# Chunked attention and a two-layer block: pairs of tiles instead of triples, softmax with a maximum, V turned on TensorE

## The chip, the cores and the metric

The kernel runs on one core of a Trainium2 chip. The metric is the device time of one execution in microseconds. TensorE multiplies matrices and transposes through a matmul with an identity; VectorE (DVE), ScalarE (ACT) and GpSimd (POOL) work on elements; POOL and SyncE (SP) also issue the DMA transfers. Every engine works through its own list of instructions in the order of the program, and waits at an instruction until what it reads or overwrites is free.

## The reference

Inputs are q, k, v of shape (4, 8, 768, 64), eight memory keys and values for each batch and head, a scale vector and two weight matrices, all in float32.

```python
chunk, left_ctx, right_ctx = (32, 16, 8)
scale = 1.0 / np.sqrt(D)
for c in range(nc):                       # 24 chunks of 32 queries
    c_start = c * chunk
    c_end = c_start + chunk
    l_start = max(0, c_start - left_ctx)
    r_end = min(S, c_end + right_ctx)
    k_full = np.concatenate([mem_k, k[:, :, l_start:r_end]], axis=2)
    v_full = np.concatenate([mem_v, v[:, :, l_start:r_end]], axis=2)
    scores = scale * np.matmul(q[:, :, c_start:c_end], k_full.transpose(0, 1, 3, 2))
    scores = scores - np.max(scores, axis=-1, keepdims=True)
    a = np.exp(scores)
    a = a / (np.sum(a, axis=-1, keepdims=True) + 1e-09)
    out[:, :, c_start:c_end] = np.matmul(a, v_full)
x = out.transpose(0, 2, 1, 3).reshape(B, S, H * D)      # (4, 768, 512)
xn = (x - mean(x)) / np.sqrt(var(x) + 1e-06) * g_ln
return x + np.maximum(xn @ w_ch1, 0.0) @ w_ch2          # hidden width 2048
```

A chunk of 32 queries sees 16 keys ahead of it, its own 32, 8 behind it, and 8 memory keys: 64 in all.

## The kernel before, in words

The 4 x 768 rows are 24 tiles of 128 rows, six for each batch. A tile is two groups of 64 rows, four chunks. An octet is eight neighbouring rows: loaded as one run of 512 numbers into one partition.

**Loads.** `load_kq` brings k and q of a batch in octets (2 KB runs). V is loaded row by row (256-byte runs) by `load_v_group` (L106) or `load_v_head` (L112); the 16 rows ahead of a group and the 8 behind it are copied from one partition to another by `v_before` and `v_after` on SP. All HBM loads stand in POOL's list, with the element work that POOL does. The weights come through `load_w1` and `load_w2`; `scale_w1` (L154) multiplies w1 by the scale vector on VectorE.

**Attention of a tile.** `kq_block` (L188, L196, L204) transposes octets of k and q on TensorE, 32 small matmuls for two heads, and copies them to `KT` (VectorE) and `QZ` (ScalarE). `scores` (L212, L219) multiplies with keys on the partitions, so that scores come out already turned for the next product; a 128-wide window of keys serves both chunks of a group, and the exponential on ScalarE, with no maximum subtracted, takes a `band` as its bias that removes the keys a chunk must not see. `values` (L231) multiplies by V, whose 65th column of ones gives the sum of the weights; VectorE divides (L238, L239) and takes mean and variance (L246, L247). `xn` is x less its mean (POOL L253 or VectorE L258); `turn_x` (L274, L279) transposes it into `xT`. POOL makes the reciprocal root of the variance (L264, L268).

**The block.** The tiles go in units: three tiles, then three units of one tile, then six of three. `up` (L291) makes 128 hidden columns for the unit with four matmuls, and relu is done on ScalarE and VectorE in turn (L297, L299). `down` (L308) makes one tile's output in 16 matmuls of 512 columns, VectorE adds the residual (L315), SP stores it.

**Order.** The order is written out by hand. A unit has 16 up steps and then four down steps for each tile; a `plan` hangs the attention of the following unit's tiles, the k and q blocks of a batch to come, and loads on these steps. PSUM holds two double banks `att` for all attention products and four banks `mm` for up and down, each used in turn.

Of the kernel before, what the change touches and what calls it, by code (L numbers as in the profile page):

```python
# [11 lines left out]
ALU = mybir.AluOpType  # L12


@with_exitstack
def kernel(
# [17 lines left out]
    KR = 104  # L34
    BLK = 72
    KC = 24 + NG * BLK + 32
    HD = 65
    CUT = 64
# [7 lines left out]
    memv16 = sb.tile([8, B, H, HD], FP16, name="memv16")  # L46
    memKT = sb.tile([128, B * 4, 8], FP16, name="memKT")
    g_col = sb.tile([128, 4], FP32, name="g_col")
    band = sb.tile([128, 2], FP32, name="band")
    zero2 = sb.tile([128, 2], FP32, name="zero2")  # L50
    ones3 = sb.tile([128, 3], FP16, name="ones3")
    hole = sb.tile([128, 1], FP16, name="hole")
    mhalf = sb.tile([128, 1], FP32, name="mhalf")
    w1c = [sb.tile([128, 4, 512], FP16, name=f"w1c{i}") for i in range(4)]
    w2c = [sb.tile([128, 4, 512], FP16, name=f"w2c{i}") for i in range(4)]
    k16 = [sb.tile([96, H, 8, 64], FP16, name=f"k16_{i}") for i in range(2)]
    q16 = [sb.tile([96, H, 8, 64], FP16, name=f"q16_{i}") for i in range(2)]
    V = [sb.tile([128, NG, H, HD], FP16, name=f"V{i}") for i in range(2)]
    KT = [sb.tile([128, 4, KC], FP16, name=f"KT{i}") for i in range(2)]
    QZ = [sb.tile([128, 4, NG, 2, 64], FP16, name=f"QZ{i}") for i in range(2)]  # L60
    AT = [sb.tile([128, 2, H, 64], FP16, name=f"AT{i}") for i in range(3)]
    xs = [sb.tile([128, 512], FP32, name=f"xs{i}") for i in range(9)]
    xn = [sb.tile([128, 512], FP16, name=f"xn{i}") for i in range(3)]
    xT = [sb.tile([128, 4, 384], FP16, name=f"xT{i}") for i in range(2)]
    rT = [sb.tile([128, 384], FP16, name=f"rT{hc}") for hc in range(16)]
    osb = [sb.tile([128, 512], FP32, name=f"osb{i}") for i in range(3)]
    bst = [sb.tile([128, 6], FP32, name=f"bst{i}") for i in range(3)]
    mv = [sb.tile([128, 2], FP32, name=f"mv{i}") for i in range(6)]
    nmean = [sb.tile([128, 1], FP32, name=f"nmean{i}") for i in range(3)]
    veps = [sb.tile([128, 1], FP32, name=f"veps{i}") for i in range(3)]  # L70
    rstd = [sb.tile([128, 1], FP32, name=f"rstd{i}") for i in range(9)]
    rec = [sb.tile([128, 2, 4], FP32, name=f"rec{i}") for i in range(2)]

    att = [ps.tile([128, 2, 512], FP32, name=f"att{i}") for i in range(2)]
    mm = [ps.tile([128, 512], FP32, name=f"mm{i}") for i in range(4)]
    turn = {"att": 0, "mm": 0}

    def slot(kind):
        lst = {"att": att, "mm": mm}[kind]
        turn[kind] = (turn[kind] + 1) % len(lst)  # L80
        return lst[turn[kind]]
# [13 lines left out]
    HS = S * D  # L95

    def load_kq(b, which, lo=0, hi=96):

        dst, src = ((k16, k), (q16, q))[which]
        nc.gpsimd.dma_start(  # L100
            out=dst[b % 2][lo:hi, :, :, :],
            in_=dram(src, b * H * HS + 512 * lo, [[512, hi - lo], [HS, H], [1, 512]]),
        )

    def load_v_group(b, g):
        nc.gpsimd.dma_start(  # L106
            out=V[b % 2][24:88, g, :, 0:64],
            in_=dram(v, b * H * HS + 64 * g * D, [[64, 64], [HS, H], [1, 64]]),
        )

    def load_v_head(b, h):
        nc.gpsimd.dma_start(  # L112
            out=V[b % 2][24:88, :, h, 0:64],
            in_=dram(v, (b * H + h) * HS, [[64, 64], [64 * 64, NG], [1, 64]]),
        )

    def load_v_after(b, g):

        nc.gpsimd.dma_start(
            out=V[b % 2][96:104, g, :, 0:64],  # L120
            in_=dram(v, b * H * HS + 64 * (g + 1) * D, [[64, 8], [HS, H], [1, 64]]),
        )

    def v_before(b, g0, g1):
        vt = V[b % 2]
        nc.sync.dma_start(out=vt[0:16, g0:g1, :, :], in_=vt[72:88, g0 - 1 : g1 - 1, :, :])

    def v_after(b, g0, g1):
        vt = V[b % 2]
        nc.sync.dma_start(out=vt[96:104, g0:g1, :, :], in_=vt[24:32, g0 + 1 : g1 + 1, :, :])  # L130

    def v_mem(b):
        vt = V[b % 2]
        src = memv16[:, b, :, :]
        nc.sync.dma_start(
            out=vt[16:24, :, :, :],
            in_=bass.AP(tensor=src.tensor, offset=src.offset,
                        ap=[list(src.ap[0]), [0, NG], [1, H * HD]]),
        )
# [12 lines left out]
    def scale_w1(c):  # L152
        for dt in range(4):
            nc.vector.tensor_scalar(  # L154
                out=w1c[c][:, dt, :], in0=w1c[c][:, dt, :], scalar1=g_col[:, dt : dt + 1],
                scalar2=None, op0=ALU.mult,
            )


    def mem_keys():  # L160
        p = slot("att")
        pv = as16(p[:, 0, :])
# [8 lines left out]
    def mem_cols(b):  # L171
        src = memKT[:, 4 * b : 4 * b + 4, :]
        nc.vector.tensor_copy(
            out=free(KT[b % 2], 16, [[KC, 4], [BLK, NG + 1], [1, 8]]),
            in_=bass.AP(tensor=src.tensor, offset=src.offset,
                        ap=[list(src.ap[0]), [8, 4], [0, NG + 1], [1, 8]]),
        )

    def kq_block(b, j, lo=0, hi=96):


        n, g0, ng = hi - lo, lo // 8, (hi - lo) // 8
        p = slot("att")
        for half, src in ((0, k16), (1, q16)):
            pv = as16(p[:, half, :])
            for r in range(8):
                for par in range(2):
                    nc.tensor.matmul(  # L188
                        out=pv[64 * par : 64 * par + 64, n * r : n * r + n],
                        lhsT=src[b % 2][lo:hi, 2 * j + par, r, :],  # L190
                        rhs=identity[lo:hi, lo:hi],
                        is_transpose=True, start=True, stop=True,
                        tile_position=(lo, 64 * par),
                    )
        pk, pq = as16(p[:, 0, :]), as16(p[:, 1, :])
        nc.vector.tensor_copy(  # L196
            out=free(KT[b % 2], j * KC + 24 + BLK * g0, [[BLK, ng], [8, 8], [1, 8]]),
            in_=free(pk, 0, [[8, ng], [1, 8], [n, 8]]),
        )
        for par in range(2):  # L200
            rows = slice(64 * par, 64 * par + 64)
            o = free(QZ[b % 2][rows, j, g0, par, :], 0, [[128, ng], [8, 8], [1, 8]])
            i = free(pq[rows, :], 0, [[8, ng], [1, 8], [n, 8]])
            nc.scalar.copy(out=o, in_=i)  # L204

    def scores(b, t):
        p = slot("att")
        a = AT[t % 3]
        for gg in range(2):
            g = 2 * t + gg  # L210
            for j in range(4):
                nc.tensor.matmul(  # L212
                    out=p[:, gg, 128 * j : 128 * j + 128],
                    lhsT=KT[b % 2][:, j, BLK * g : BLK * g + 128],
                    rhs=QZ[b % 2][:, j, g, :, :],
                    start=True, stop=True,
                )
        for c in range(2):
            nc.scalar.activation(  # L219
                out=free(a, 32 * c, [[512, 2], [64, 8], [1, 32]], KR),  # L220
                in_=free(p, 32 * c, [[512, 2], [64, 8], [1, 32]], KR),
                func=ACTF.Exp, bias=band[0:KR, c : c + 1], scale=0.125,
            )

    def values(b, t, xi, on_pool):
        x = xs[xi]
        p = slot("att")
        for h in range(H):
            for gg in range(2):
                c0 = HD * (h % 4)  # L230
                nc.tensor.matmul(  # L231
                    out=p[64 * gg : 64 * gg + 64, h // 4, c0 : c0 + HD],
                    lhsT=AT[t % 3][0:KR, gg, h, :],
                    rhs=V[b % 2][0:KR, 2 * t + gg, h, :],
                    start=(h % 4 == 0), stop=(h % 4 == 3), tile_position=(0, 64 * gg),
                )
        r = rec[t % 2]
        nc.vector.reciprocal(out=r, in_=free(p, 64, [[512, 2], [HD, 4]]))  # L238
        nc.vector.tensor_tensor(  # L239
            out=x.rearrange("p (a h d) -> p a h d", a=2, h=4),  # L240
            in0=free(p, 0, [[512, 2], [HD, 4], [1, 64]]),
            in1=free(r, 0, [[4, 2], [1, 4], [0, 64]]),
            op=ALU.mult,
        )
        i, m = t % 3, mv[t]
        nc.vector.bn_stats(out=bst[i], in_=x)  # L246
        nc.vector.bn_aggr(out=m, in_=bst[i])  # L247
        if on_pool:
            nc.gpsimd.tensor_scalar(  # L249
# [53 lines left out]
    def down(t, i, part):  # L303
        if part == 0:
            down_slot[i] = slot("mm")
# [82 lines left out]
    for c in range(4):  # L388
        load_w1(c)
# [161 lines left out]
```

## Time and profile before

| what | value |
|---|---|
| device time, median of 3 runs | 278.22 us (277.54 to 278.29) |
| span of the profiled execution, first to last instruction | 277.4 us |
| TensorE busy | 231.5 us (83%) in 2480 matmuls |
| VectorE, ScalarE, GpSimd busy | 148.9, 91.1, 80.4 us |
| moved by DMA | 21.87 MB in 40,491 packets, 28,064 of them under 512 bytes |
| mean granted TensorE clock | 0.960 |

The profiled execution's own time is known as its span only; the runs lie 0.1 to 0.9 us above it. PE is TensorE's matmuls, PEld its weight loads, which overlap with them. Busy times are sums over one execution; "idle before" in a row is the time that the engine stood ahead of such an instruction, with what ended it.

### The profile page before, as it was taken

The page shows a single profiled execution, that of the slowest core. Times are in us where ns is not written, and L with a number is a line of the kernel's source. Part 1 is how long each engine was busy: PE and PEld are TensorE (multiplying, and loading weights), DVE is VectorE, ACT ScalarE, POOL GpSimd, SP SyncE. Part 2 cuts the span into 40 slices and gives each one's busy share as a digit, 9 for nine tenths or more (in the row PEclk, how much of TensorE's full clock was granted, in tenths as well). Part 3 has the DMA queues.
Part 4 walks back from the last instruction along what each step waited for, and adds up shares of the span by engine and source line. Part 5 has one row for each costly group of instructions (what it writes and reads, how often), then busy time and mean ns, then how long its engine had stood idle before and what let it go on. Part 6 is the DMA issues. An engine that isn't in the chain of part 4 may idle for free.

```text
span 277.4 us, 5949 instructions
## 1 busy us (share of the span) xinstructions
PE 231.5 (83%) x2480; PEld 143.3 (52%) x2480; DVE 148.9 (54%) x300; ACT 91.1 (33%) x177; POOL 80.4 (29%) x161
## 2 busy tenths in 40 slices
PE   0255592789919797789999999999999999999993
PEld 0254341345615657357655764666467557646641
DVE  6837658922614754954665555465636446553411
ACT  1074021141300457137344540376234305501300
POOL 6593240000605260370760224053402221320000
PEclk9999999668986999999999999999999999999998
DMA  6999996000694399079979801627950021012002
GB/s 54 146 125 212 213 187 66 0 2 2 80 228 31 73 120 55 2 118 191 67 85 160 182 0 51 94 15 34 95 119 0 2 77 38 4 38 78 0 38 76
DMA packets 40491, 21.87 MB, mean 79 GB/s; under 512 B 28064, under 2 KB 36672, under 8 KB 40416
## 3 DMA queue, kind: packets, MB, share of 16 engines
q0 software_dynamic: 35584, 13.72, 51.4%
q1 hardware_dynamic: 4880, 7.78, 9.8%
q8 instruction: 19, 0.31, 0.4%
q14 instruction: 8, 0.07, 0.1%
HBM read 27.43 MB, written 6.29 MB: 122 GB/s over the span
## 4 chain that ended last, share of the span: by engine, by line
PE 70%; DVE 17%; ACT 4%; DMA 4%; issue 3%; POOL 1%; DVEq 0%; ACTq 0%
PE mm L291 29%; PE mm L308 28%; PE att L188 5%; DMA V<-in_v_dram 4%; DVE V L334 4%; PE att L212 3%; PE att L231 3%; ACT QZ L204 3%; DVE bst L246 2%; DVE xs L239 2%; PE att L274 1%; ACT AT L219 1%; DVE KT L196 1%; DVE osb L315 1%; DVE w1c L154 1%
## 5 line engine op out<-in xcount | busy, mean ns | idle before, releaser
L291 PE MATMUL mm<-xT,w1c 128*128 128x384 f16 (+1 forms) x640 | 98.6, 305 | 11.8 <-DVE w1c L154 7.4
L308 PE MATMUL mm<-w2c,rT 128*128 128x512 f16 x384 | 93.7, 393 | 0.0
L291 PEld LDWEIGHTS <-w1c 128*128 128x128 f16 x640 | 61.3, 116 | 37.8 <-DVE w1c L154 9.0
L297 ACT ACTIVATE rT<-mm 128x384 f16<-128x384 f32 (+1 forms) x80 | 33.5, 427 | 118.1 <-PE mm L291 75.5
L308 PEld LDWEIGHTS <-rT 128*128 128x128 f16 x384 | 36.3, 100 | 40.0 <-issue 5.0
L299 DVE TENSOR_SCALAR rT<-mm 128x384 f16<-128x384 f32 (+1 forms) x80 | 37.3, 471 | 34.1 <-PE mm L291 33.9
L204 ACT COPY QZ<-att 64x512 f16<-64x512 f16 (+2 forms) x48 | 27.8, 579 | 43.9 <-DVE KT L196 43.3
L315 DVE SCALAR_TENSOR_TENSOR osb<-mm,rstd,xs 128x512 f32<-128x512 f32 x24 | 18.0, 750 | 30.5 <-PE mm L308 24.8
L219 ACT ACTIVATE AT<-att,band 104x512 f16<-104x512 f32 x48 | 30.2, 683 | 9.3 <-PE att L212 9.1
L249 POOL TENSOR_SCALAR nmean<-mv 128x1 f32<-128x1 f32 x15 | 2.8, 189 | 87.0 <-DVE mv L247 52.6
L196 DVE COPY KT<-att 128x512 f16<-128x512 f16 (+2 forms) x24 | 16.5, 689 | 16.0 <-PE att L188 13.0
L264 POOL TENSOR_SCALAR veps<-mv 128x1 f32<-128x1 f32 x24 | 6.3, 262 | 59.6 <-DVE mv L247 58.2
L106 POOL DMA_DIRECT2D V<-in_v_dram x24 | 16.6, 697 | 14.0 <-DMA w1c<-in_moe_w_ch_dram 4.6
L212 PE MATMUL att<-QZ,KT 128*128 128x128 f16 x192 | 16.3, 233 | 3.4 <-ACT QZ L204 2.9
L279 DVE COPY xT<-att 128x512 f16<-128x512 f16 x24 | 10.1, 419 | 14.2 <-PE att L274 14.1
L231 PE MATMUL att<-V,AT 104*64 104x65 f16 x384 | 11.7, 206 | 6.6 <-DMA V<-in_v_dram 5.8
L246 DVE BATCH_NORM_STATS2 bst<-xs 128x6 f32<-128x512 f32 x24 | 16.7, 694 | 0.8
L239 DVE TENSOR_TENSOR xs<-att,rec 128x512 f32<-128x512 f32 x24 | 16.6, 691 | 0.8
L212 PEld LDWEIGHTS <-KT 128*128 128x128 f16 x192 | 13.9, 105 | 5.9 <-issue 3.8
L188 PE MATMUL att<-identity,k 64*64 64x64 f16 (+2 forms) x384 | 12.1, 203 | 5.7 <-DMA k<-in_k_dram 2.4
L238 DVE RECIPROCAL rec<-att 128x8 f32<-128x8 f32 x24 | 4.8, 202 | 21.8 <-PE att L231 21.8
L188 PEld LDWEIGHTS <-k 64*64 64x64 f16 (+2 forms) x384 | 10.0, 116 | 12.0 <-issue 6.9
(48 smaller groups left out, 140.1 us busy)
## 6 DMA issues: line engine op xcount, KB each, us to landing
out_dram<-osb SPq DMA_DIRECT2D x24, 256.0 KB
w1c<-in_moe_w_ch_dram POOLq DMA_DIRECT2D x4, 512.0 KB, 8.8
w2c<-in_moe_w_ch_dram POOLq DMA_DIRECT2D x4, 512.0 KB, 15.2
V<-in_v_dram POOLq DMA_DIRECT2D x24, 64.0 KB, 7.4
k<-in_k_dram POOLq DMA_DIRECT2D x2, 768.0 KB, 11.4
q<-in_q_dram POOLq DMA_DIRECT2D x2, 768.0 KB, 14.9
V<-in_v_dram POOLq DMA_DIRECT2D x16, 96.0 KB, 4.5
k<-in_k_dram POOLq DMA_DIRECT2D x2, 512.0 KB, 6.4
```

What stands on the lines that cost most here:

```text
L188: nc.tensor.matmul(out=pv[64 * par : 64 * par + 64, n * r : n * r + n], lhsT=src[b % 2][lo:hi, 2 * j + par, r, :], rhs=identity[lo:hi, lo:hi],
L204: nc.scalar.copy(out=o, in_=i)
L212: nc.tensor.matmul(out=p[:, gg, 128 * j : 128 * j + 128], lhsT=KT[b % 2][:, j, BLK * g : BLK * g + 128], rhs=QZ[b % 2][:, j, g, :, :], sta ...
L219: nc.scalar.activation(out=free(a, 32 * c, [[512, 2], [64, 8], [1, 32]], KR), in_=free(p, 32 * c, [[512, 2], [64, 8], [1, 32]], KR), func= ...
L231: nc.tensor.matmul(out=p[64 * gg : 64 * gg + 64, h // 4, c0 : c0 + HD], lhsT=AT[t % 3][0:KR, gg, h, :], rhs=V[b % 2][0:KR, 2 * t + gg, h, ...
L239: nc.vector.tensor_tensor(out=x.rearrange("p (a h d) -> p a h d", a=2, h=4), in0=free(p, 0, [[512, 2], [HD, 4], [1, 64]]), in1=free(r, 0, ...
L246: nc.vector.bn_stats(out=bst[i], in_=x)
L291: nc.tensor.matmul(out=p, lhsT=free(w, i, [[4, 128]]), rhs=xT[u % 2][:, dt, 0 : 128 * n], start=(dt == 0), stop=(dt == 3),)
L297: nc.scalar.activation(out=o, in_=p, func=ACTF.Relu)
L299: nc.vector.tensor_scalar(out=o, in0=p, scalar1=0.0, scalar2=None, op0=ALU.max)
L308: nc.tensor.matmul(out=p, lhsT=rT[hc][:, 128 * i : 128 * i + 128], rhs=w2c[hc // 4][:, hc % 4, :], start=(hc == 0), stop=(hc == 15),)
L315: nc.vector.scalar_tensor_tensor(out=o, in0=p, scalar=rstd[t % 9], in1=xs[t % 9], op0=ALU.mult, op1=ALU.add,)
```

## The change

The kernel is written anew around the same products.

- **Pairs.** All units are pairs of tiles, so up's moving operand is 256 columns wide (before 384 or 128). Steps of `up` for a pair alternate with steps of `down` for the pair before it. Up has two banks, down two, attention two single banks (`one`) and one double bank (`two`). All relus run on ScalarE, for two hidden blocks at once.
- **Softmax.** `qk` makes scores with queries on the partitions, for each chunk exactly its 64 keys. VectorE takes the maximum over the keys and subtracts it; ScalarE's exponential needs no bias. `pt` transposes the weights on TensorE; VectorE and ScalarE copy one half each into `PTz`, whose other halves stay zero. `KT` keeps the keys in a stream where memory keys lie between the others, so that a chunk's keys are 64 neighbours.
- **Statistics.** The division also gives the row's sum; the sum of squares is a Square with an accumulator on ScalarE, with its bias from POOL's `nmean`.
- **V.** Of the first batch, V is loaded in octets, and transposed twice on TensorE (`turn_stream`, `v_turn`) into its place. `VT`, its form between, lies in the second batch's `KT`. The other batches load V row by row, with the shared rows loaded from HBM twice (`load_v_group` has two DMAs); `v_shared` copies 24 rows inside the chip.
- **First weights.** The first four tiles have the scale vector in `xn`, on VectorE; w1 is scaled on POOL during unit 1, with clears for the second batch.

```diff
-            nc.vector.tensor_scalar(          # scale_w1
+            nc.gpsimd.tensor_scalar(
                 out=w1c[c][:, dt, :], in0=w1c[c][:, dt, :], scalar1=g_col[:, dt : dt + 1],
...
+    def turn_stream(dst, i, j, o0, lo, n, engine):
+        pv = turn(i, j, lo, n)                # 16 transposes into one bank
+        ng, g0 = n // 8, o0 // 8
+        for first, cnt, at in ((0, 2, 16), (2, 6, 40)):
+            copy_on(engine)(
+                out=free(dst, j * KC + at + BLK * g0, [[BLK, ng], [8, cnt], [1, 8]]),
+                in_=free(pv, first, [[8, ng], [1, cnt], [n, 8]]),
+            )
...
+    def v_turn(g, vt, engine):
+        p = slot()
+        pv = as16(p)[:, 0:512]
+        for j in range(4):
+            for y in range(2):
+                lo = BLK * g + 32 * y
+                nc.tensor.matmul(
+                    out=pv[64 * y : 64 * y + 64, 128 * j : 128 * j + 128],
+                    lhsT=vt[:, j, lo : lo + 64], rhs=identity,
+                    is_transpose=True, start=True, stop=True, tile_position=(0, 64 * y),
+                )
...
+    def qk(t):
+        p = slot()
+        for y in range(2):
             for j in range(4):
+                for gg in range(2):
+                    g = 2 * tt + gg
+                    nc.tensor.matmul(
+                        out=p[64 * gg : 64 * gg + 64, 128 * j + 64 * y : 128 * j + 64 * y + 64],
+                        lhsT=QZ[b % 2][:, j, 2 * g + y, :, :],
+                        rhs=KT[b % 2][:, j, BLK * g + 32 * y : BLK * g + 32 * y + 64],
+                        start=True, stop=True, tile_position=(0, 64 * gg),
+                    )
+        m, s = nmx[t % 2], sub[t % 2]
+        nc.vector.tensor_reduce(out=m, in_=scores, axis=AX.X, op=ALU.max)
+        nc.vector.tensor_tensor(out=s, in0=scores, in1=m, op=ALU.subtract)
+        nc.scalar.activation(out=P[t % 3], in_=s, func=ACTF.Exp, scale=0.125)
+    def pt(t):
+        for j in range(4):                    # transposes of P into a bank, then
+        nc.vector.tensor_copy(out=z[0:64, :, 0, :], in_=src[0:64, :, :])
+        nc.scalar.copy(out=z[64:128, :, 1, :], in_=src[64:128, :, :])
+    def val(t, w1_scaled=True):
+        # 16 matmuls of PTz and V into the bank two, then
+        nc.vector.reciprocal(out=r, in_=free(two, 64, [[128, 8]]))
+        nc.vector.tensor_tensor_reduce(... op0=ALU.mult, op1=ALU.add, accum_out=xsum[i])
+        eng = nc.gpsimd if w1_scaled else nc.vector
+        eng.tensor_scalar(out=nmean[i], in0=xsum[i], scalar1=-1.0 / 512, ...)
+        # xn: POOL (x + nmean), or VectorE (x + nmean) * g_row
+        nc.scalar.activation(
+            out=sq, in_=x, func=ACTF.Square, bias=nmean[i], scale=1.0, accum_out=ssq[i],
+        )
+        nc.gpsimd.tensor_scalar(out=veps[i], in0=ssq[i], ...)
+        nc.gpsimd.tensor_tensor(out=rstd[t % 9], in0=veps[i], in1=mhalf, op=ALU.pow)
...
+    for u in range(1, NP - 1):
+        a, c = 2 * u + 2, 2 * u + 3
+        at(u, 0 if u > 1 else 1, qk, a)
+        at(u, 2, qk, c)
+        at(u, 4, pt, a)
+        at(u, 6, val, a)
+        at(u, 7, pt, c)
+        at(u, 9, val, c)
+        at(u, 11, turn_x, a)
+        at(u, 14, turn_x, c)
+    at(1, 6, clear_q, 1, nc.gpsimd)
+    at(1, 8, ready_v, 1, nc.gpsimd)
+    for c in range(4):
+        at(1 + c // 3, (4, 8, 12, 0)[c] , scale_w1, c)
...
+            at(1, 3, load_kq, b)              # batch 1
             for j in range(4):
+                at(1, 9 + 2 * j, turn_stream, KT[1], 0, j, 0, 0, 96, "V")
+                at(1, 9 + 2 * j, turn_q, 1, 1, j, 0, 0, 96, "AA")
+            for g in range(NG):
+                at(1, 8 + g // 2, load_v_group, 1, g)
...
+            at(u0 - 1, 1, load_kq, b)         # batches 2 and 3, u0 = 3 * b - 3
             for j in range(4):
+                w, s = u0 + j // 2, 8 if j % 2 == 0 else 12
+                at(w, s, turn_stream, KT[b % 2], 0, j, 0, 0, 96, "V")
+                at(w, s, turn_q, b, 1, j, 0, 0, 96, "AA")
+            for h in range(H):
+                for part in range(2):
+                    at(u0, 2 * h, load_v_head, b, h, part)
...
+    for u in range(1, NP):
+        for step in range(16):
+            for fn, args in plan.get((u, step), ()):
+                fn(*args)
+            if step % 2 == 0:
+                up(u, step // 2)
             else:
+                down(u - 1, step // 2)
+    for part in range(8):
+        down(NP - 1, part)
```

Ahead of this loop stands unit 0's up, with the attention of tiles 0 and 1 before it and that of tiles 2 and 3 between its steps. Some calls above are written shorter than they are.

## The prediction

> **What bounds the kernel now.** I read the 40 slices first, to see which engine is full and when.
>
> ```profile
> PE   0255592789919797789999999999999999999993
> DVE  6837658922614754954665555465636446553411
> PEclk9999999668986999999999999999999999999998
> DMA  6999996000694399079979801627950021012002
> ```
>
> From slice 17 (118 us) TensorE is full; before that it is idle for about 40 us. The DMA engines are full up to 42 us. The clock falls after TensorE's gaps. The stretches give numbers to that (columns: length, then busy us and count of PE, PEld, DVE, ACT, POOL, granted clock, DMA share in tens of us, GB/s).
>
> ```profile
> 40.00:50.00 10.00, 3.09 (x16) 1.74 (x16) 8.31 (x13) 1.32 (x3) 1.81 (x5) 0.86 0.62 80
> 50.00:60.00 10.00, 8.78 (x148) 5.38 (x149) 6.58 (x15) 3.91 (x10) 0.00 (x0) 0.67 0.01 2
> 220.00:240.00 20.00, 20.00 (x169) 12.27 (x167) 11.24 (x23) 5.81 (x11) 3.24 (x8) 1.00 0.11 41
> ```
>
> The chain that ended last names the early gaps and prices the late part:
>
> ```profile
> 42.17 5.26 DVE V L334
> 72.10 10.75 DMA V<-in_v_dram
> 137.14 0.82 PE att L188 x32
> 203.80 1.30 PE mm L291 x8
> 228.07 1.30 PE mm L291 x8
> 252.35 10.40 PE mm L291 x64
> 262.75 10.37 PE mm L308 x48
> 273.20 0.75 DVE osb L315
> ```
>
> Six tiles are finished at 119.3 us, late for a V memset and a V load. The other 18 take 154.6 us, 8.6 a tile, and TensorE sets them. The unit from 203.80 to 228.07 has 24.3 us for three tiles: 10.4 up, 10.4 down, 3.5 attention (1.17 a tile). Prices of small work come from the groups by shape:
>
> ```profile
> L297 ACT ACTIVATE rT<-mm 128x384 f16<-128x384 f32 x56 | 27.3, 490 | 92.7 <-PE mm L291 50.1 <-DVE rT L299 42.2
> L219 ACT ACTIVATE AT<-att,band 104x512 f16<-104x512 f32 x48 | 30.2, 683 | 9.3 <-PE att L212 9.1
> L239 DVE TENSOR_TENSOR xs<-att,rec 128x512 f32<-128x512 f32 x24 | 16.6, 691 | 0.8
> L106 POOL DMA_DIRECT2D V<-in_v_dram x24 | 16.6, 697 | 14.0 <-DMA w1c<-in_moe_w_ch_dram 4.6 <-DVE V L340 3.3 <-DMA w2c<-in_moe_w_ch_dram 3.3
> L253 POOL TENSOR_SCALAR xn<-xs,nmean 128x512 f16<-128x512 f32 x15 | 10.4, 692 | 1.5
> ```
>
> **A pair in the steady state.** a and c are the two tiles that a unit prepares. Up: 64 matmuls of 256 columns. None is in the trace; between 128 columns (20 in 1.12 us, 56 ns) and 384 (64 in 10.40, 163 ns) lies 109 ns, so 7.0 us. Down: 32 x 216 ns = 6.9. qk: 16 matmuls of 64 columns in two column halves, like values' 16 of 65 in 0.38 us. Transposed weights: 4 like turn_x, 0.22. Values 0.38, turn_x 0.22. A tile has 1.2 against the old 1.05; with 0.1 for switching the pair is 13.9 + 2.6 = 16.5 us.
>
> DVE has per tile: maximum (not in the trace; between 0.42, a 512-wide f16 copy, and 0.75, L315; taken like L246, 0.69), subtraction 0.69, copy 0.42, reciprocal 0.20, product with its sum 0.75, xT 0.42, residual 0.75: 7.8 a pair, hidden under 16.5. ACT has eight relus of 512 (0.60 by the slope from 128 to 384), two exps 0.61, two copies 0.58, two squares 0.8: 8.8, hidden on average. But it runs in order. From a unit's start: exp(a) ends at 2.65, relu 0 at 3.25, exp(c) 4.75, relu 1 5.35, copy(a) 5.9, relu 2 6.5, square(a), which waits for POOL's nmean, 8.95, relu 3 9.55, copy(c) 10.1. TensorE reaches val(c) at 9.5 and waits 0.7. Plain unit: **17.2**.
>
> A unit with two k/q blocks adds 2 x 0.80 of transposes. There are only two `one` banks left: turn_q needs the bank whose last reader is copy(c), so it waits 1.2 us (and val(c) then none): **19.3**. Bounds are the work alone, 16.5 and 18.1, and one more ACT operation late, 18 and 20.5. Units 3, 4, 6, 7 are of this kind, 5, 8, 9, 10 plain; unit 11 has no attention, 14.0.
>
> **Start, to unit 1.** V in octets takes 6144 small packets out of the first loads. q0's 35,584 packets took 51.4% of 16 engines x 277.4 = 2281 us; about 10,000 are of 2 KB or its equal; at 90 ns for these the small ones cost 55. So 6144 x 55 / 16 = 21 us less DMA, and the 5.26 us memset L334 is gone. What comes in its place is a chain through DVE and ACT: clears to 7.7; memory keys and four K copies (0.25 + 0.45 each) to 11.6; q copies; ready_v (3.1) and memory values to 16.5; maximum, subtraction, exp(0) 18.6; V's copies on ACT 21.2; v_turn, weights, val(0) 24; xn(0) 26.1; the same for tile 1, 30.8; xT 31.8. First up at 31.9 (before: 31.7): the DMA gain is hidden behind this chain. Four ups 3.6; then k, q, V blocks of 32 octets (2.8, 2.2, 2.8 of DVE through two banks), qk(2), qk(3), v_turns, val(2), val(3), each with rec to xn of 2.2 on DVE: unit 1 begins at **55** (50 with no gaps between DVE's operations, 59 with 0.2 more each).
>
> **Unit 1 and POOL's queue.** POOL gets scale_w1 (16 x 0.69 by L253; before 16 x 0.35 on DVE), the clears for batch 1, and 24 V loads (two a group where before were 12 and copies). It runs in order, and val(5)'s nmean stands behind the work of steps 6 to 8. From the unit's start: k, q, V rests through two banks and DVE, up, qk(4), qk(5), val(4) at 13.5; nmean(4) 14.9, its four operations to 16.8; clear_q: two memsets of 1536 words (slope 0.6 ns on POOL's small memsets, 0.87 on DVE's L348: 0.9 to 1.34 each; 1.2 taken) 19.2; ready_v: 2944 elements, 2.5, 21.7; scale_w1(1) 3.0 with gaps, 24.7; four V issues 2.6 (0.59 to 0.70 each): 27.3. Only then nmean(5). ACT stands at square(5) meanwhile; behind it are block 0's q copies (1.6) and relu 5. They end at 30; turn_stream(1) wants a bank that these copies read, and TensorE, in order, has come there at 20.5. Stall 9.5. The remaining ups, downs and three k/q blocks, paced by ACT's q copies, take 7: 37. Row and clock: after the idle 43.4 to 50.3 the clock was 0.60 to 0.74 up to 65 us, and 12 downs took 5.23 instead of 2.59; after a wait of 5.8 us the stretch 83 to 90 had 0.63. This loses 2.6 to 5.5 us; part falls in ACT's time, so 3: unit 1 is **40** (35 to 45).
>
> The Trainium skill (TensorE: Matmul & The Clock Gate, Part 1) has full rate back after about 3.4 us of sustained work. An estimate by that page would lose 1.7 us and end the kernel 1.3 us earlier. The 15 us in this trace speak against the rule here, as the work after the gap is itself broken.
>
> **Unit 2.** It waits about 1 us for the last q copy. POOL still has V issues and scale_w1(3) to about 50 us after unit 1's start, where nmean(6) is wanted at 47: 3 us. 17.2 + 4 = **21** (17 to 25). V of groups 0 to 3 lands, at 55 ns a packet, some 4 us before val(6).
>
> **Sum.** 55 + 40 + 21 + 4 x 19.3 + 4 x 17.2 + 14.0 + last down 6.9 + tail 4.3 (273.1 to 277.4 before) = 287.2. That stands against the span 277.4; the runs' median is 278.22, 0.8 above it. So **288 us**. Against before: unit 3 begins at 116 with a pair's down (6.9) still owed, 122.9 where before stood at 119.3; the other 18 tiles take 160 instead of 154.6; the tail has 4.3 behind the last matmul. Those are the 10 us.
>
> **Rivals.**
> *The start really shortens, faster.* The one mechanism is slack in DVE's start chain: transposes and copies run ahead. It decides if unit 1 begins below 48 and hence val(4) comes at 11. For it: DVE spent the first 13 us before on clears, and TensorE was idle for 40. Then 47 + 36 + 19 + 4 x 18.1 + 4 x 16.7 + 25.2 = 266.4, so 267. Against it: every first tile is a serial path over five engines. Chance 0.24.
> *The load queue blocks again.* V of a batch now has 8256 packets (28 us of DMA at 55 ns) instead of 6144, issued from POOL in one unit of 19; if POOL waits for old loads to land, as it did for w1c (4.6 us in three waits), nmean is late in units 3 and 6 too, some 5 us and 1 of clock each: 300. Chance 0.22.
> *It comes out even.* Half of unit 1's stall (4.8) and half the start's slack (4): 279; chance 0.04.
> The forecast has 0.50.
>
> **Numbers.** A measurement of this kernel tells 0.3%, 0.8 us, from no change. Range 269 to 304: from just above the faster rival to the blocked queue with a late start; leaves out 2 in 10. The slower cases alone (0.72) lie between 281 and 304. Faster 0.24, same 0.04, slower 0.72.
>
> The Trainium skill (GPSIMD Engine Reference, section 4.1) puts one-input work on GpSimd near line rate, so it would not mind scale_w1 there; L253 and L154 say 0.69 against 0.35.
>
> **What would show it.** Right: POOL's longest stretch of work without a gap lies in unit 1; ACT's longest wait is Square on POOL's nmean; TensorE has a gap of 7 to 11 us near 75 us with a clock near 0.6 after it; matmuls of 256 columns follow each other at 109 ns; plain units take 17.2. Wrong: unit 1 starting under 48; Square never waiting over 2 us; steady units under 16.5; TensorE waiting for a V load; a second table load on ACT (0 assumed; one is 1.28 us, two a tile would be 60 us).

## The result and the profile after

The changed kernel takes 308.84 us (median of 4 runs, 307.82 to 309.10) where the kernel before took 277.88 beside it: ratio 1.109, 95% interval 1.104 to 1.113. The profiled execution has a span of 306.1 us (before 277.4) and a mean granted clock of 0.928 (before 0.960). The direction was forecast; the size was not, 31 us instead of 10.

The 40 slices of the changed kernel, to be laid against those of before:

```profile
PE   0545787879950794998998999989899999999994
DVE  7284347464430261444355543555445354442001
POOL 8323000030499997454914227185220403022000
PEclk9999985585995699899999999999999999999999
DMA  7999940049002889991953794469230100000101
```

A slice is 7.65 us, and they are counted from 0. In slices 11 and 12 TensorE goes from 5 to 0, and the clock falls to 0.5 and 0.6 (12 and 13); just there POOL stands at 9, in slices 11 to 14. Ahead of it, in slices 5 to 9, the clock is down although TensorE is at 7 to 9. The 4 in slice 15 is a second, shorter wait; from slice 16 on TensorE is at 8 or 9. The stretches give numbers (columns as in the prediction): the first 32 ups, unit 1 as a whole, the ten microseconds of the gap, a plain unit.

```profile
34.55:40.82 6.27, 6.27 (x36) 4.42 (x37) 0.00 (x0) 1.79 (x3) 0.00 (x0) 1.00 1.23 171
63.79:110.98 47.19, 31.99 (x531) 22.33 (x530) 16.98 (x50) 17.21 (x31) 31.72 (x46) 0.75 0.48 56
90.00:100.00 10.00, 0.00 (x0) 0.00 (x0) 0.00 (x0) 0.80 (x3) 9.52 (x15) 0.56 0.25 16
229.37:246.70 17.33, 16.83 (x177) 12.01 (x176) 7.67 (x16) 8.39 (x16) 3.26 (x8) 1.00 0.09 32
```

From 90 to 100 us POOL works 9.52 us, ScalarE 0.80, TensorE and VectorE nothing. The waits name the chain (engine and line, what it waited for, us in total, times, longest):

```profile
ACT sq L340 <- POOL nmean L328: 44.3, 20, 13.4
PE one L226 <- ACT QZ L250: 13.1, 1, 13.1
PE two L313 <- DMA V<-V: 4.2, 1, 4.2
```

And the timeline shows it instruction by instruction (start, duration):

```profile
85.01 2.65 POOL L401 MEMSET QZ<- 64x3072 f16 x1
87.71 2.65 POOL L402 MEMSET QZ<- 64x3072 f16 x1
90.42 1.38 POOL L405 MEMSET V<- 128x1536 f16 x1
...
93.61 2.71 POOL L169 TENSOR_SCALAR w1c<-w1c,g_col 128x512 f16<-128x512 f16 x4
...
98.96 0.21 POOL L328 TENSOR_SCALAR nmean<-xsum 128x1 f32<-128x1 f32 x1
99.20 0.72 ACT L340 ACTIVATE sq<-xs,nmean 128x512 f16<-128x512 f32 x1 [13.36 <-POOL nmean L328]
...
99.93 1.58 ACT L250 COPY QZ<-one 64x768 f16<-64x768 f16 x2
```

A scaling of 128 numbers, 0.21 us of work, stands in POOL's list behind 14 us of clears, scalings and load issues for the next batch. Square on ScalarE waits for it, the q copies stand behind Square, and TensorE waits for these copies.

By place, the 28.7 us of the two spans divide so: unit 3 begins at 133.65 with 6.9 of down owed, so the first six tiles end at 140.6 where before they ended at 119.3 (+21.3); the last residual ends at 302.9, 162.3 later, where before 154.6 went by (+7.7); the tail gives 0.3 back.

### The profile page after: what moved, and what is told of

It reads as the page before. It is cut to its first block, busy times and chain, and to the rows that moved or that the text cites. A ratio compares the mean times of both kernels' runs of the same rounds, so it can differ in the third digit from the quotient of the medians.

```text
span 306.1 us, 7397 instructions
## 1 busy us (share of the span) xinstructions
PE 252.3 (82%) x3192; PEld 180.2 (59%) x3192; DVE 132.6 (43%) x313; ACT 131.2 (43%) x243; POOL 113.7 (37%) x203
## 4 chain that ended last, share of the span: by engine, by line
PE 42%; issue 19%; POOL 15%; ACT 9%; DVE 8%; DMA 6%; SPq 1%; DVEq 0%; POOLq 0%; ACTq 0%
PE upb L371 16%; PE dnb L386 14%; PE one L226 4%; ACT sq L340 4%; POOL V L123 4%; DMA raw<-in_q_dram 3%; POOL V L128 3%; DMA V<-V 3%; PE two L313 2%; POOL rstd L347 2%; ACT QZ L250 2%; DVE xs L321 2%; PE one L280 1%; ACT PTz L307 1%; PE one L262 1%
## 5 line engine op out<-in xcount | busy, mean ns | idle before, releaser
L371 PE MATMUL upb<-xT,w1c 128*128 128x256 f16 x768 | 107.4, 287 | 0.5 <-DVE xT L359 0.5
L386 PE MATMUL dnb<-w2c,rT 128*128 128x512 f16 x384 | 99.5, 386 | 0.0
L371 PEld LDWEIGHTS <-w1c 128*128 128x128 f16 x768 | 82.6, 118 | 13.5 <-issue 1.4
L377 ACT ACTIVATE rT<-upb 128x512 f16<-128x512 f32 x96 | 56.6, 590 | 36.7 <-PE upb L371 36.1
L226 PEld LDWEIGHTS <-raw 96*64 96x64 f16 (+3 forms) x960 | 25.0, 127 | 30.1 <-issue 25.4
L226 PE MATMUL one<-identity,raw 96*64 96x96 f16 (+3 forms) x832 | 25.1, 203 | 21.2 <-ACT QZ L250 13.1
L340 ACT ACTIVATE sq<-xs,nmean 128x512 f16<-128x512 f32 x24 | 17.4, 724 | 51.2 <-POOL nmean L328 44.3
L250 ACT COPY QZ<-one 64x768 f16<-64x768 f16 (+3 forms) x36 | 23.4, 651 | 25.6 <-PE one L226 25.1
L393 DVE SCALAR_TENSOR_TENSOR xs<-dnb,rstd,xs 128x512 f32<-128x512 f32 x24 | 18.0, 750 | 33.6 <-PE dnb L386 33.6
L240 DVE COPY KT<-one 128x192 f16<-128x192 f16 (+4 forms) x56 | 18.7, 380 | 30.9 <-PE one L226 30.6
L313 PEld LDWEIGHTS <-PTz 128*64 128x64 f16 x384 | 8.7, 117 | 18.6 <-ACT PTz L307 9.1
## 6 DMA issues: line engine op xcount, KB each, us to landing
raw<-in_q_dram POOLq DMA_DIRECT2D x3, 768.0 KB, 10.7
w1c<-in_moe_w_ch_dram POOLq DMA_DIRECT2D x4, 512.0 KB, 15.4
w2c<-in_moe_w_ch_dram POOLq DMA_DIRECT2D x4, 512.0 KB, 16.5
```

What stands on the lines that cost most here:

```text
L226: nc.tensor.matmul(out=pv[64 * par : 64 * par + 64, n * r : n * r + n], lhsT=raw[i][lo : lo + n, 2 * j + par, r, :], rhs=identity[lo : lo ...
L240: copy_on(engine)(out=free(dst, j * KC + at + BLK * g0, [[BLK, ng], [8, cnt], [1, 8]]), in_=free(pv, first, [[8, ng], [1, cnt], [n, 8]]),)
L250: copy_on(engines[par])(out=free(QZ[b % 2][rows, j, c0, par, :], 0, [[64, ncn], [8, 4], [1, 8]]), in_=free(pv[rows, :], 0, [[4, ncn], [1, ...
L313: nc.tensor.matmul(out=two[64 * gg : 64 * gg + 64, 128 * h : 128 * h + 65], lhsT=PTz[t % 3][:, 4 * (h // 2) + 2 * gg + h % 2, :, :], rhs=V ...
L340: nc.scalar.activation(out=sq, in_=x, func=ACTF.Square, bias=nmean[i], scale=1.0, accum_out=ssq[i],)
L371: nc.tensor.matmul(out=p[:, 256 * hb : 256 * hb + 256], lhsT=free(w1c[hc // 4][:, dt, :], hc % 4, [[4, 128]]), rhs=xT[u % 3][:, dt, :], st ...
```

## The experiments

Below, "unit 2 begins" is the first product of `qk(6)`: 110.98 us in the changed kernel. All edits are edits of the changed kernel, and all ratios are to the kernel before.

**The mean on VectorE.** Only the small operation leaves POOL's list; all the bulk work stays.

```diff
-        eng = nc.gpsimd if w1_scaled else nc.vector
+        eng = nc.vector
```

> Only nmean of every tile goes from POOL to VectorE. Theory (POOL's backlog reaches TensorE through ScalarE, which stands at Square on nmean and holds the q copies and relus behind it): the 13.1 us gap of TensorE in unit 1 shrinks to 4 to 6 us, since xn of tile 5 stays behind the same backlog; some 2 us of the gain go into a longer wait for V in unit 2; 308.8 falls to about 302. Rival (the backlog is felt through V's late loads and xn, ScalarE's wait is a symptom): within 2 us of 308.8.

Measured: 298.63 us, ratio 1.074 (1.072 to 1.076), 10.2 less than the changed kernel; unit 2 begins at 102.87. The waits now begin so:

```profile
POOL xn L333 <- DVE nmean L328: 94.2, 17, 12.8
```

POOL waits for VectorE, not ScalarE for POOL. The wait of 13.1 on TensorE is gone, and a shorter one stands in its place, for POOL's `xn` behind the same bulk work:

```profile
PE one L353 <- POOL xn L333: 5.9, 1, 5.9
```

Steady units stay at 17.3 and 19.6. So the place of the small operation made the long wait, and the amount of POOL's work still costs the shorter one. Of the 8.1 us by which unit 2 begins earlier, 1.5 lie ahead of unit 1, in a start that the edit leaves as it was; the filler products below come back to that.

**The clears early.** The same list, relieved from the other side: the two clears for batch 1 stand in the start instead of steps 6 and 8 of unit 1.

```diff
+    clear_q(1, nc.gpsimd)      # right after banks["list"] = one
+    ready_v(1, nc.gpsimd)
...
-    at(1, 6, clear_q, 1, nc.gpsimd)
-    at(1, 8, ready_v, 1, nc.gpsimd)
```

> The clears for batch 1 (two memsets of 2.65 us on QZ, 3.0 us on V) stay on POOL but stand ahead of unit 0's first up, where POOL is idle for 24 us. Theory: they are 8.3 us of the 13.1 us gap and leave it; gap 4 to 5 us, V of batch 1 lands earlier by the same, 308.8 falls by 8 to 10 us to about 299.5. Rival (the clock and the small steps of unit 1 set its length, the gap moves elsewhere): 305 or more.

Measured: 299.22 us, ratio 1.076 (1.073 to 1.079). Unit 2 begins at 102.38, and Square's longest wait is 6.0 instead of 13.4, and TensorE's wait for the q copies 4.5 instead of 13.1. The clears alone were worth 9.6 us.

**POOL free in unit 1.** As well as the clears, the V loads of batch 1 go ahead of unit 1 and the scaling of w1 goes to VectorE.

```diff
+    for g in range(NG):
+        load_v_group(1, g)     # behind the two clears
...
-            nc.gpsimd.tensor_scalar(          # scale_w1
+            nc.vector.tensor_scalar(
```

> As the run with early clears, and the V loads of batch 1 also stand ahead of unit 0's first up, and w1 is scaled on VectorE at the same steps. Theory: POOL holds nothing but the tiles' own small operations in units 1 and 2; no gap over 2 us in unit 1, no wait for V in unit 2; unit 1 falls from 47.2 to about 32, unit 2 from 22.7 to 17.5, the whole to about 289. What is left over the kernel before (about 11 us) is then the start to 63.8 and the steady units. Rival (the clock decides): unit 1 stays over 38, the whole over 296.

Measured: 296.38 us, ratio 1.066 (1.062 to 1.070): only 2.8 below the kernel with the clears alone. Unit 2 does begin at 95.13, 7.2 earlier than there, but itself takes 26.0 us. Why stands in its timeline:

```profile
109.43 0.65 PE L313 MATMUL two<-V,PTz 128*64 128x65 f16 x16 [7.30 <-DMA V<-V]
```

The copies of V's shared rows inside the chip are still issued where unit 2 begins, at 96 to 98 us, and land 11 us later. The wait did not vanish; it moved to what was next.

**The copies early too.** The kernel above, with `v_mem` and `v_shared` of batch 1 in unit 1.

```diff
-            at(2, 0, v_mem, 1)
+            at(1, 3, v_mem, 1)
...
-                at(2, g // 4, v_shared, 1, g, g + 4)
+                at(1, 4 + g // 4, v_shared, 1, g, g + 4)
```

> As e3_pool_free, and the copies that complete V of batch 1 (v_mem, v_shared on SP) stand in unit 1, steps 3 to 6, instead of unit 2, steps 0 to 2. In e3 val(6) waited 7.3 us for them: issued at 96 to 101, they landed at 109.4 while k and q of batch 2 were coming in. Theory: the wait goes, unit 2 becomes 17.3 to 18.5 from 26.0, the whole falls from 296.4 to about 288. Rival (the copies wait for V's own loads, so they land no earlier): within 2 us of 296.4.

Measured: 287.36 us, ratio 1.033 (1.029 to 1.037). Unit 2 takes 17.6 (97.14 to 114.76). The clears, the loads, the scaling and the copies, placed elsewhere, give back 21.5 us of the changed kernel's time, where the clears alone gave 9.6 and the first three 12.5.

**Weights on VectorE.** Is the rest above 16.5 in a steady unit ScalarE's order?

```diff
-        nc.scalar.copy(out=z[64:128, :, 1, :], in_=src[64:128, :, :])
+        nc.vector.tensor_copy(out=z[64:128, :, 1, :], in_=src[64:128, :, :])
```

> Both halves of the transposed weights are copied by VectorE; nothing else changes. Theory (in the steady units ScalarE's order of work makes val(c) and the second k/q block's bank wait): plain units 17.3 become 16.8, k/q units 19.6 become 18.5, the whole falls by 6 to 7 us to about 302. Rival (TensorE's own work and switches fill the units): units unchanged within 0.2, the whole 308 to 309.

Measured: 301.19 us, ratio 1.081 (1.076 to 1.086). A unit with two k/q blocks and a plain one:

```profile
130.65:149.26 18.61, 18.61 (x242) 13.34 (x242) 10.48 (x22) 10.39 (x18) 10.86 (x19) 1.00 0.65 66
167.86:184.62 16.76, 16.76 (x179) 12.03 (x178) 8.52 (x18) 7.22 (x14) 5.93 (x12) 1.00 0.79 125
```

TensorE is busy all the time in both: 18.6 and 16.8 against 19.6 and 17.3. The stalls by ScalarE's order were 1.0 and 0.6 us, near the 1.2 and 0.7 assumed.

**No maximum.** Maximum and subtraction are left out; the exponential reads the scores in their bank.

```diff
-        nc.vector.tensor_reduce(out=m, in_=scores, axis=AX.X, op=ALU.max)
-        nc.vector.tensor_tensor(out=s, in0=scores, in1=m, op=ALU.subtract)
-        nc.scalar.activation(out=P[t % 3], in_=s, func=ACTF.Exp, scale=0.125)
+        nc.scalar.activation(out=P[t % 3], in_=p, func=ACTF.Exp, scale=0.125)
```

> The maximum and its subtraction are left out; ScalarE takes the exponential straight from the scores in PSUM (softmax without the maximum gives the same quotient). Theory: the two VectorE operations (1.4 us a tile) are hidden in the steady units, 17.3 and 19.6 stay within 0.3; in the serial start each of the four tiles shortens the chain by up to 1.4, so unit 1 begins 3 to 5 us earlier, near 60; the whole 303 to 306. Rival (VectorE's added work costs in every unit, as a reduction there is slow): units fall by over 0.5, the whole below 300.

Measured: 302.80 us, ratio 1.087 (1.081 to 1.091). `qk(4)` comes at 64.67 instead of 72.16; unit 3 takes 19.6 and unit 5 17.3, as with the maximum. So the operation costs something in the start, where tiles follow each other in series, and nothing that shows in the steady state. Not all of the 6.0 us need be its own: in the trace unit 1 begins 7.8 us earlier (55.97 instead of 63.79), more than the 1.4 us of each of four tiles, as the first 32 ups also took 4.77 us instead of 6.27.

**Filler matmuls in the start.** The first ups run at little more than half the later rate (6.27 us for 32, 196 ns each instead of 109). Does that make the start long? Products of 512 columns that nobody reads are put between the steps of the start; they write the second of down's banks.

```diff
+    def filler(n):
+        for _ in range(n):
+            nc.tensor.matmul(out=dnb[1], lhsT=identity, rhs=heat, start=True, stop=True)
```

> 64 matmuls of 512 columns on a tile of ones are put between the start's TensorE steps, ahead of unit 1, into a down bank that nobody reads yet; the start's rotation has five banks instead of six. Theory 1 (the clock alone cost what the start has over the forecast, 63.8 against 55): with the clock at full the first 32 ups take 3.5 us instead of 6.3, unit 0's later ups 0.9 instead of 1.8 each, unit 1 begins at 57 to 59, the whole 303 to 305. Theory 2 (the start is a chain through VectorE and ScalarE, TensorE's rate hardly matters): unit 1 begins at 61 or later, the whole 306 to 310.

Measured: 309.43 us, ratio 1.112 (1.109 to 1.116). The first ups do run close to the full rate (timeline, start and duration):

```profile
35.73 3.66 PE L376 MATMUL upb<-xT,w1c 128*128 128x256 f16 x32 [0.15 <-DVE xT L364]
```

But `qk(4)` comes at 73.02, not before 72.16. The fillers themselves stand in the way: from the end of these ups to up step 4 TensorE is never idle and takes 15.4 us, where the changed kernel took 11.5 with gaps. So this run does not tell what the rate costs. Two other runs tell more, as they have the same program up to unit 1: the changed kernel, and the one with the mean on VectorE.

```profile
34.55 6.27 PE L371 MATMUL upb<-xT,w1c 128*128 128x256 f16 x32 [0.52 <-DVE xT L359]
...
34.87 4.90 PE L371 MATMUL upb<-xT,w1c 128*128 128x256 f16 x32 [0.51 <-DVE xT L359]
```

The second begins its ups 0.3 us later and runs them 1.4 faster; it is 1.2 ahead at up step 4 (51.04 against 52.27) and 1.5 at unit 1 (62.34 against 63.79). What the first ups lose to the slow rate is passed on. How long a start at the full rate throughout would be, no run shows.

**V of the first batch by rows.** The octets and their turning are undone for batch 0: `load_v_group`, `v_mem` and `v_shared` as in the other batches.

```diff
-    load_octets(2, v, 0, 0, 48, 0)
+    for g in range(4):
+        load_v_group(0, g)
...
-    for i, src in enumerate((k, q, v)):
+    for i, src in enumerate((k, q)):
...
-    for j in range(4):
-        turn_stream(VT, 2, j, 0, 0, 48, "A")
-    v_turn(0, VT, "V")
-    v_turn(1, VT, "V")
```

> V of batch 0 by rows as for batch 1 (two loads a group, v_mem and v_shared), no octets of V, no turning on TensorE; ready_v(0) stands ahead of the first k copies. Theory (the turning sits on the serial start, while the DMA it saves was hidden): first up at 30 to 32 instead of 34.6, unit 1 begins at 57 to 60 and has 4 to 5 us less small work, the whole 297 to 302. Rival (V in octets pays: 28 us of small packets among the first loads make the weights late): first up or up 4 waits for w1, the whole 309 or more.

Measured: 293.92 us, ratio 1.056 (1.051 to 1.061), 14.9 less. The first up comes at 31.5 instead of 34.55, unit 1 begins at 53.1 instead of 63.79, and unit 2 at 94.99 instead of 110.98. In unit 1 POOL's list is as it was, and so is the wait for it:

```profile
ACT sq L340 <- POOL nmean L328: 43.5, 20, 13.3
```

The transfer that octets save is more than lost: 10.7 us in the start and 5.3 in unit 1, where their last block is turned. That is more than the theory gave. Some 2.3 of the 10.7 are ups that ran faster here (those of unit 0 took 10.2 us in all instead of 12.5).

**All of it.** Mean, scaling and the second half of the weights on VectorE; V of batch 0 by rows; the clears on POOL between the first V loads; half of batch 1's V loads ahead of `val(4)`, its copies, all but the last, in unit 1. The maximum stays. The lines that the experiments above do not show:

```diff
+    load_v_group(0, 4)
+    load_v_group(0, 5)
+    clear_q(1, nc.gpsimd)
+    load_v_group(0, 6)
+    load_v_group(0, 7)
+    ready_v(1, nc.gpsimd)
...
-                at(1, 8 + g // 2, load_v_group, 1, g)
+                at(1, 4 if g < 6 else 9 + (g - 6) // 2, load_v_group, 1, g)
...
-                at(2, g // 4, v_shared, 1, g, g + 4)
+                at(1 + g // 8, (7, 12, 0)[g // 4], v_shared, 1, g, g + 4)
```

> All that helped, with the maximum kept: V of batch 0 by rows, both halves of the transposed weights copied by VectorE, nmean and w1's scaling on VectorE, batch 1's clears on POOL between the first loads, half of batch 1's V loads ahead of val(4), and its copies in unit 1. From the runs: unit 1 begins near 53 (e8), has no gap over 3 us and takes 27 to 30, unit 2 takes 17 to 19 (e6), later units 18.6 and 16.8 (e4): 53 + 28.5 + 18 + 4 x 18.6 + 4 x 16.8 + 25 = 266. Theory (the rewrite's loss lies in these waits, its pairs are sound): 264 to 270, faster than before's 278. Rival (the gains overlap, POOL's loads of both batches collide and one wait takes another's place): 275 or more.

Measured: 271.21 us (271.07 to 272.30), ratio 0.975 (0.971 to 0.979): faster than both kernels. Unit 2 begins at 86.85. What is late now, in the timeline of ScalarE and of TensorE:

```profile
56.17 0.72 ACT L340 ACTIVATE sq<-xs,nmean 128x512 f16<-128x512 f32 x1 [7.03 <-POOL veps L343]
...
57.99 1.02 PE L226 MATMUL one<-identity,raw 16*64 16x16 f16 x32 [5.06 <-DVE QZ L250]
```

Square, again: its sum goes into one of three buffers, which POOL's `veps` must have read, and this stands behind V loads that wait for their turn.

**All of it, without the maximum.** The same, with maximum and subtraction left out as before.

```diff
-        nc.vector.tensor_reduce(out=m, in_=scores, axis=AX.X, op=ALU.max)
-        nc.vector.tensor_tensor(out=s, in0=scores, in1=m, op=ALU.subtract)
-        nc.scalar.activation(out=P[t % 3], in_=s, func=ACTF.Exp, scale=0.125)
+        nc.scalar.activation(out=P[t % 3], in_=p, func=ACTF.Exp, scale=0.125)
```

> As e9_all_max, without the maximum and its subtraction. Theory: as in e5 the start gets 4 to 6 us shorter and the units stay; 260 to 265. Rival (with V by rows the start waits for V and the weights, not for VectorE): within 1.5 us of e9.

Measured: 272.03 us, ratio 0.976 (0.970 to 0.981), no different from 271.21. What the maximum cost is now hidden in the start too: unit 1 begins at 51.28 against 51.65, and `qk(4)` comes at 62.47 against 62.88. The chains that ended last name what stands ahead in both: copies of V inside the chip, which land at 24.0 and 24.5, and POOL's list with `veps` behind V loads before `qk(4)`.

**Nine buffers for the sum of squares,** in the kernel with all of it and the maximum.

```diff
-    ssq = [sb.tile([128, 1], FP32, name=f"ssq{i}") for i in range(3)]
+    ssq = [sb.tile([128, 1], FP32, name=f"ssq{i}") for i in range(9)]
...
-            out=sq, in_=x, func=ACTF.Square, bias=nmean[i], scale=1.0, accum_out=ssq[i],
+            out=sq, in_=x, func=ACTF.Square, bias=nmean[i], scale=1.0, accum_out=ssq[t % 9],
```

> As e9_all_max, with nine buffers for the sum of squares instead of three. In e9 ScalarE stood 7.0 us at Square of tile 3 (49.1 to 56.2), since veps of tile 0, which reads the same buffer, stood on POOL behind batch 0's V loads; TensorE waited 5.1 us of it for a q copy. Theory (POOL's list reaches TensorE over any small buffer that ScalarE shares with it): the wait goes, unit 1 begins its first up 4 to 6 us earlier, the whole 265 to 268. Rival (k and q of batch 1, issued by POOL after those loads, are what unit 1 waits for): within 1.5 us of 271.2.

Measured: 272.03 us, ratio 0.980 (0.974 to 0.987). The wait of 7 is gone and `qk(4)` comes at 57.92 instead of 62.88, yet unit 2 begins at 86.94. The chain that ends last has for this stretch:

```profile
59.24 0.85 POOL raw L101
60.09 14.18 DMA raw<-in_q_dram
```

Five microseconds won, and waited for again at the next load: batch 1's queries were sent for at the same moment as before and landed at 74.3.

**These loads earlier.** In the kernel of nine buffers, two further ones for raw k and q let batch 1's be sent for behind batch 0's last V loads.

```diff
+    load_octets(2, k, 1, 0, 96, 0)      # in the start
+    load_octets(3, q, 1, 0, 96, 0)
...
-            at(1, 3, load_kq, b)
```

> The kernel of nine ssq buffers, with two further buffers for raw k and q, so that batch 1's k and q are sent for in the start, behind batch 0's last V loads, and not in unit 1 once batch 0's blocks have been transposed. In the kernel of nine ssq buffers unit 1's qk(4) came at 57.92 instead of 62.88 but unit 2's qk(6) still at 86.94 (86.85): the queries of batch 1, sent for at about 60.3, landed 14.2 us later, at 74.6. Theory: that load is what unit 1 waits for now; then unit 1 has its work alone left (29 us down to 22 to 25), qk(6) comes at 80 to 83 and the time is 264 to 268. Rival: the DMA engines or POOL's order are the limit, and V of batch 0 or 1, or batch 1's loads, come as late in any order: within 1.5 of 272.0. Plain units stay at 16.8, those with two k/q blocks at 18.6.

Measured: 269.37 us (268.48 to 271.81), ratio 0.973 (0.964 to 0.982). Unit 2 begins at 84.70, between what the theory and the rival gave, and the interval covers the two kernels above, so no gain over them is shown. In the trace the loads went out only 4.1 us earlier, as POOL's list stood behind w2's transfers, and two waits remain:

```profile
70.75 0.53 PE L226 MATMUL one<-identity,raw 96*64 96x96 f16 x16 [1.63 <-DMA raw<-in_q_dram]
...
74.92 0.40 PE L353 MATMUL one<-identity,xn 128*128 128x128 f16 x4 [1.80 <-POOL xn L333]
```

## Why the prediction was right or wrong

**Mechanism of the stall, right.** POOL's longest unbroken stretch begins in unit 1 (83.1 to 120.9, on into unit 2), Square waits there for `nmean`, and TensorE stands behind it. The first two experiments show it from both sides, by moving the small operation and by moving the bulk. The gap is longer and later than named: 13.1 us from 88.5, not 7 to 11 near 75.

**Steady units, right.** 17.3 and 19.6 us against 17.2 and 19.3; eight ups of 256 columns take 0.87 us, 109 ns each; from unit 10's begin to the end 42.2 against 42.4 (17.2 and 25.2). There is one table load, as assumed. The rival in which the load queue blocks units 3 and 6 again is out: they take 19.6 like units 4 and 7.

**The start, mis-sized by 8.8** (63.79 instead of 55). I had taken the octets' DMA gain as hidden, which is right: with rows the first up comes earlier, not later. Two terms of the sum failed. One is the serial chain in which V's turning stands: with rows in place of octets the start is 10.7 shorter, more than the whole miss. The other is the rate of the ups: the sum has all ups of the start at the full rate, and charges the low clock to unit 1 alone. Of the 8.8, 2.7 lie before the first up, 2.7 in the first 32 ups (6.27 instead of 3.6) and 3.5 behind them, with tiles 2 and 3 and the second V blocks. On the chain that ended last, three of the later up steps stand with 1.83, 1.83 and 1.20 us instead of 0.87; with the first 32 the slow rate makes some 4.9 of the 8.8 (an estimate from these rows). How the rest and this would divide without each other, no run shows, as the ups ran faster with rows too.

**Unit 1, mis-sized by 7.2** (47.2 instead of 40). `nmean(5)` was to end its wait 27.3 after the unit's start; it came 35.2 after it. Of these 7.9, 4.4 come before the clears: POOL reached them 21.2 into the unit, not 16.8. Two up steps of eight products and a down step of four took 1.82 to 1.83 us each under the low clock, where the full rate needs 0.87: 2.9 of the 4.4. I had charged the clock to the unit's end only. The other 3.5 are mainly two memsets, taken at 1.2 each and lasting 2.65. (Behind the wait, 0.7 came back.) I priced them by words of 32 bits. The groups by shape of the changed kernel (busy, mean ns) say otherwise:

```profile
L402 POOL MEMSET QZ<- 64x3072 f16 x1 | 2.7, 2653 | 0.1
...
L405 POOL MEMSET V<- 128x1536 f16 x1 | 1.4, 1383 | 0.1
...
L401 DVE MEMSET QZ<- 64x1536 uint32 x1 | 1.3, 1338 | 0.3 <-issue 0.3
...
L405 DVE MEMSET V<- 128x1536 f16 x1 | 1.3, 1338 | 0.4 <-issue 0.4
```

The price of these goes by elements: 0.87 ns each on VectorE, with 16 bits or 32, and 0.86 to 0.90 on POOL, where the clears of `QZ` have halfwords as elements. The Trainium skill (VectorE: DVE Perf Modes, section "Zero memsets can be issued as uint32 (trn2)") says of VectorE that a memset takes a cycle an element whatever the type; its two rows here agree. Of POOL the page does not speak, and POOL's rows have 16 bits only.

**Unit 2, right size, wrong cause** (22.7 instead of 21). I put 3 us of waiting on POOL's `nmean` and had V landing 4 us before it was wanted. It landed late: `val(6)` waited 4.2 for the copies inside the chip. I had counted the packets of the HBM loads and not the time from issue to landing of the copies (7.7 us from 113.94 here, 11.1 in the third experiment).

**Rest.** These three make 17.7; 1.2 more are in steady units, and the median lies 2.7 above the profiled span, not 0.8. Every run of the changed kernel lies 1.7 above its own span, and the profiled one was the quickest of the four.

**The faster rival** put unit 1's start below 48. It is wrong as it stands, at 63.8, yet the corrected kernel has something of it: unit 1 begins at 51.65 there, the first six tiles end at 111.0 (before 119.3), and the other 18 take 156.3 (before 154.6). So even the mended version owes its whole gain to the first six tiles and loses a little in the steady state. What bounds its unit 1 is left open between the loads of batch 1 and POOL's list: the last experiment moved both a little.

## What to carry to other kernels

Engines that work through lists in order are coupled by small results: ahead of moving bulk work to an idle engine, look for a tiny operation in its list that another engine waits for, and place the bulk behind it. A transfer that is already hidden saved nothing when shortened here, and what replaced it in a serial start was paid for. A test that adds work has to be read with the time of that work: the filler products hid what they gained. When a wait is taken away, cost the next one before counting the gain; here copies, buffers and loads took its place in three kernels in turn.

## What the hardware showed unexpectedly

The granted clock reads 1.00 from 34.55 to 40.82 us while 32 products of 256 columns take 6.27 us, 196 ns each, against 109 later; with filler products ahead they take 114. The column seems to hold 1.00 until the record has its first change (here after 43 us), so there the rate of the matmuls is the better reading. The Trainium skill (TensorE: Matmul & The Clock Gate, Part 1) has TensorE start at half rate until it has been busy for about 3.4 us. The two rates fit that. The time lies on both sides of the page's figure: with no break between the products, they quicken near 39.6 in the changed kernel, 5.0 us after the first, and near 37.4 with the mean on VectorE, 2.5 us after it.
